# A planned attention and two-FFN kernel: pairs of PSUM banks taken early, and new numbers for the planner's pools and due times

## The chip, the core and the metric

One of the eight cores of a Trainium2 chip runs the whole program. The metric is device time in microseconds, start to end of the one launch. Its engines are PE (TensorE, matmuls), ACT (ScalarE), DVE (VectorE), POOL (GpSimd) and SP (SyncE, which only issues DMAs). Each runs its own list of instructions in the order in which they were written, and waits on semaphores for the others.

## What is computed

```
attention, per batch (2 batches of 12288 queries, C = 128):
  kv_pool = mean of 4x4 patches of kv           -> 768 keys
  k = v   = kv_pool @ w_sr
  x1      = softmax(q @ k.T / sqrt(C)) @ v
layer 1:  h = x1 @ w_in1 (128 -> 2048);  g = h * clip(h + 3, 0, 6) / 6;  x2 = g @ w_out1
layer 2:  h = x2 @ w_in2 (128 -> 2048);  g = h * cos(h);                 out = g @ w_out2
```

Inputs and output are float32.

## The kernel before

**Tiles.** The 24576 queries are cut into 48 blocks `b` of 512. A layer of a block is 8 units `p`; a unit is 256 of the 2048 hidden features, which fill a pair of PSUM banks (2 x 512 floats in each partition). Every float32 operand of a matmul is split into two float16 halves, `hi` and `lo`, and a product is three matmuls: hi·hi, lo·hi, hi·lo.

**A unit**, by its operations and lines: `ff_in` (PE, six matmuls of 512 columns, L1141 to L1143, into a pair of banks); in layer 1 `relu` (ACT, L1156) and `gate` (DVE, L1161), after which the pair is free; in layer 2 `turns` (ACT, L1166), `rest` (DVE, L1171), `sine` (ACT, L1177) and `times` (DVE, L1180), after which the pair is free; then `cast` to float16 `hi` (on ACT, L1186, or on POOL, L1188, whichever the planner finds sooner), `low` (POOL, L1191) and `ff_out` (PE, six matmuls, L1149 to L1151, into a single bank that gathers all 8 units of the block). Layer 2 runs 28 units behind layer 1 (`LAG`).

**Attention of a block.** Four `scores` (PE, L896, six matmuls each, into a pair of banks), each followed by `row_max` (DVE, L901 and L905) and `exp` (ACT, L911). Then there are two ways to turn the exponentials round for the product with the values:

- blocks below `BY_PE`: PE transposes them (`by_pe`, L999), ACT or DVE copies them out, and `values` (L1029) multiplies in float32; the queries are transposed by PE too (L778);
- all other blocks: DVE splits them into halves (`split`, L970 and L971), which frees the pair; SP stores them to DRAM (`store`, L977, tile `scr`), reads them back with three transposing DMAs (L1014, one for each third of the keys), and `values` (L1035) is three groups of six float16 matmuls, one behind each DMA. The queries go the same way (`power` and `up`, L796 to L818, `split` on POOL, L830 and L831, then DMAs).

**What sets the order.** The kernel is written as a list of about 8000 operations. `Plan.run` is a list scheduler that runs while the program is built: it walks through time with a fixed cost for every operation, gives each engine the ready operation of the lowest `prio` whose tiles are free, and so writes every engine's list. `prio` is the block's due time plus the offsets in the table of constants (`AV_AT` for `values`, `OUT_AT` for `ff_out`, and so on); operations more than `WINDOW` beyond the oldest open one may not start. Tiles come from pools of fixed size: `NW` float32 tiles, `NHI`, `NLO` and `NY` float16 ones, and the eight PSUM banks of the class `Banks`, from which an operation takes one bank or two neighbouring ones. On the chip nothing of this is decided again: only the lists and the semaphores are left.

Of the kernel before, what the change touches and what calls it, by code (L numbers as in the profile page):

```python
# [36 lines left out]
LAG = 28  # L37
AHEAD = 4

NW, NHI, NLO, NY = 16, 18, 18, 11  # L40
SPARE = 5

NSCR = 3

BY_PE = 6

VALUES = [[0], [1], [2]]

NBANKS = 8

NSUM = 5

# [6 lines left out]
TURNS = 2  # L59

POOL_PARTS = 16
RAWS = 8
ET_SPARE = 2

FIRST_SPARE, FIRST_BLOCKS = 0, 6


WINDOW = 150000.0
LOAD_AHEAD = 5000
Q_AHEAD = 20000  # L70
KV_AHEAD, KV_STEP, KV_PROJECT = 400000, 110000, 20000
KV_FIRST = 40000
IDLE_UNTIL = 10
WARM = 3
A_STEP = 1000
W_FIRST, W_STEP = 8000.0, 6000.0
HI_AT, LO_AT, OUT_AT = 12000, 8000, 20000
OUT_STEP = 1800
Q_AT, AT_AT, AV_AT, XS_AT = -1000, 4000, 20000, 20000
ACT_AT, DVE_AT, SIN_AT, MUL_AT = 4000, 200, -6000, -8000  # L80


BANKS = {"one": 1, "two": 2}
# [17 lines left out]
class Banks:  # L101
# [5 lines left out]

    def __init__(self, n):
        self.free = [True] * n

    def find(self, n):
        f = self.free
        if n == 1:
            at = [i for i in range(len(f)) if f[i]]
            return min(at, key=lambda i: (f[i ^ 1], i), default=None)
        at = [i for i in range(len(f) - 1) if f[i] and f[i + 1]]
        return max(at, key=lambda i: (i % 2 == 0, i), default=None)

    def pop(self, n):
        i = self.find(n)  # L120
        self.free[i : i + n] = [False] * n
        return i, n

    def append(self, taken):
        i, n = taken
        self.free[i : i + n] = [True] * n


class Plan:
# [24 lines left out]

    def lacks(self, tag, spare):
        if tag in BANKS:
            return self.slots[tag].find(BANKS[tag]) is None
        return len(self.slots[tag]) <= spare

# [3 lines left out]
    def run(self):  # L163
# [19 lines left out]
        events = [0.0]  # L183
# [4 lines left out]
        now = 0.0  # L188
        while started < len(self.ops):
            assert events, [  # L190
                (o.prio, o.where, o.take) for o in order if o not in begun and not todo[o]
            ][:20]
            now = max(now, heapq.heappop(events))
            while backs and backs[0][0] <= now:
                _, _, key = heapq.heappop(backs)
                tag, tile_ = self.held.pop(key)
# [5 lines left out]
            while again:  # L202
                again = False
                for e in sorted(queue):
# [3 lines left out]
                    while queue[e]:  # L208
                        item = heapq.heappop(queue[e])
                        o = item[2]  # L210
# [25 lines left out]
                    o = pick  # L236
# [16 lines left out]
                    heapq.heappush(events, o.end)  # L253
                    for key in o.drop:
                        heapq.heappush(backs, (o.seen, o.seq, key))
                    for u in users.get(o, ()):
                        todo[u] -= 1
                        if not todo[u]:
                            ready(u, max(a.seen for a in u.after))
                            heapq.heappush(events, ready_at[u])  # L260
# [4 lines left out]
def attention_ffn_ffn_kernel(  # L265
# [54 lines left out]

    free_banks = Banks(NBANKS)
    plan = Plan(
# [23 lines left out]

    banks = psum.tile([P, NBANKS, T], F32, name="banks")

# [415 lines left out]
    def plan_attention(prio, b):  # L764
# [80 lines left out]

        if b < BY_PE:
            a = op(prio - LOAD_AHEAD, {"dma": 1400}, load, take=[(raw, "w")])
# [16 lines left out]
        for j in range(NJ):  # L864
            a = plan_scores(prio + 1000 * j, b, j, [q_op, *k_ops], by_op)
            if b >= BY_PE:
                a, stored = plan_halves(prio + 1000 * j + 500, b, j, a, first)
# [7 lines left out]
        a = None  # L875
        for cps in [[cp] for cp in range(GK)] if b < BY_PE else VALUES:
            cp = cps[0]
            before = [a, *(parts[c] for c in cps)]
            if not cp:
                before += [v_32[0], v_32[1]] if b < BY_PE else v_ops  # L880
            a = plan_values(prio + AV_AT + 1300 * cp, b, cps, before, acc)
# [3 lines left out]
    def plan_scores(prio, b, j, before, by_op):  # L885
# [24 lines left out]
        def exp(e):  # L910
            nc.scalar.activation(  # L911
                flat(plan[e_])[:, 0:KEYS] if b < BY_PE else keys_of(ps), keys_of(ps), AF.Exp,
                bias=plan[nm][:, 0:1], scale=plan["qs", b][:, 2:3],
# [499 lines left out]
```

## Time and profile before

| | us |
|---|---|
| device time, median of 3 runs | 2563.74 (2561.98 to 2566.88) |
| device time of the profiled execution | 2567.5 |
| its span, first to last instruction | 2565.7 |
| PE busy | 2459.1 (96%) |
| ACT, DVE, POOL busy | 2256.9, 2203.1, 2080.4 |

A matmul's row in the trace is as long as the matmul is in the pipeline, longer than the distance to the next one's start. Where PE waits, the next row names in brackets how long the engine had no row, and who ended that.

### The profile page before, as it was taken

What the parts mean: (1) busy time and instruction counts of PE and PEld (TensorE: products, weight loads), DVE (VectorE), ACT (ScalarE), POOL (GpSimd) and SP (SyncE); (2) the same over time, 40 slices, a digit from 0 to 9 for tenths busy, and PEclk for the clock granted to TensorE, in tenths of its full rate; (3) what the DMA queues carried; (4) which work ended last, traced back from release to release, by engine and by line L of the source; (5) the groups of instructions that cost most, each with busy time, mean ns of one, the idle gap of its engine ahead of it and who ended that gap; (6) DMA issues with size and microseconds to landing.
All of it is one profiled execution on the core that took longest, in us unless ns stands there. A gap on an engine that the chain in (4) does not pass through costs nothing.

```text
span 2565.7 us, 33121 instructions
## 1 busy us (share of the span) xinstructions
PE 2459.1 (96%) x11616; PEld 1147.2 (45%) x11616; DVE 2203.1 (86%) x2775; ACT 2256.9 (88%) x2485; POOL 2080.4 (81%) x1231
## 2 busy tenths in 40 slices
PE   7999999999999999999999999999999999999998
PEld 5444444444444444444444444444444444444443
DVE  8977898888888888888888888889888888888887
ACT  4889888889888888898898989989998899988898
POOL 1998787888778787788778887888788888876888
PEclk9999999999999999999999999999999999999999
DMA  6201334553555334543345344543553455334401
GB/s 214 62 21 46 78 91 101 114 119 75 135 112 108 102 83 103 103 107 79 89 103 113 87 91 109 108 84 91 112 111 78 91 112 110 74 81 95 92 13 42
DMA packets 553514, 239.86 MB, mean 93 GB/s; under 512 B 370049, under 2 KB 524801, under 8 KB 553345
## 3 DMA queue, kind: packets, MB, share of 16 engines
q1 hardware_dynamic: 553344, 237.73, 41.1%
q8 instruction: 91, 1.49, 0.3%
q14 instruction: 79, 0.64, 0.1%
HBM read 46.20 MB, written 102.07 MB: 58 GB/s over the span
## 4 chain that ended last, share of the span: by engine, by line
PE 39%; DVE 18%; ACT 18%; DMA 13%; issue 6%; POOL 3%; SPq 3%; ACTq 0%; DVEq 0%; POOLq 0%
DMA w<-scr 8%; DVE w L1161 5%; PE banks L1149 5%; PE banks L1151 5%; PE banks L1150 5%; PE banks L1141 5%; PE banks L1143 5%; PE banks L1142 5%; DMA scr<-w 4%; PE banks L1035 4%; ACT w L1166 3%; ACT hi L1186 3%; ACT banks L911 3%; ACT w L1156 3%; PE banks L896 3%
## 5 line engine op out<-in xcount | busy, mean ns | idle before, releaser
L1191 POOL TENSOR_TENSOR lo<-w,hi 128x1024 f16<-128x1024 f32 x768 | 1620.8, 2136 | 154.4 <-ACT hi L1186 148.1
L1186 ACT CAST hi<-w 128x1024 f16<-128x1024 f32 x554 | 572.5, 1044 | 115.1 <-DVE w L1161 93.9
L1141 PE MATMUL banks<-y,w_in_hi 128*128 128x512 f16 x1536 | 583.3, 380 | 30.7 <-DVE w L1180 14.6
L1151 PE MATMUL banks<-lo,w_out_hi 128*128 128x512 f16 x1536 | 583.1, 380 | 8.5 <-POOL lo L1191 8.4
L1149 PE MATMUL banks<-hi,w_out_hi 128*128 128x512 f16 x1536 | 583.0, 380 | 3.2 <-DVE w L1180 2.3
L1142 PE MATMUL banks<-y,w_in_lo 128*128 128x512 f16 x1536 | 583.0, 380 | 0.0
L1143 PE MATMUL banks<-y,w_in_hi 128*128 128x512 f16 x1536 | 583.0, 380 | 0.0
L1150 PE MATMUL banks<-hi,w_out_lo 128*128 128x512 f16 x1536 | 582.7, 379 | 0.0
L1171 DVE SCALAR_TENSOR_TENSOR w<-banks,by,w 128x1024 f32<-128x1024 f32 x384 | 488.3, 1280 | 87.6 <-ACT w L1166 82.9
L1180 DVE SCALAR_TENSOR_TENSOR w<-w,banks 128x1024 f32<-128x1024 f32 x384 | 463.6, 1217 | 102.5 <-ACT w L1177 98.5
L1161 DVE SCALAR_TENSOR_TENSOR w<-w,banks 128x1024 f32<-128x1024 f32 x384 | 464.3, 1214 | 71.7 <-ACT w L1156 71.1
L1156 ACT ACTIVATE w<-banks,three,v_by 128x1024 f32<-128x1024 f32 x384 | 459.5, 1202 | 29.8 <-PE banks L1143 24.5
L1166 ACT ACTIVATE w<-banks,by 128x1024 int32<-128x1024 f32 x384 | 422.1, 1110 | 65.2 <-PE banks L1143 46.3
L1177 ACT ACTIVATE w<-w,quarter 128x1024 f32<-128x1024 f32 x384 | 436.2, 1148 | 21.6 <-DVE w L1171 14.8
L1188 POOL CAST hi<-w 128x1024 f16<-128x1024 f32 x214 | 220.7, 1039 | 206.5 <-PE banks L1151 85.5
L1142 PEld LDWEIGHTS <-w_in_lo 128*128 128x128 f16 x1536 | 150.2, 98 | 217.2 <-issue 56.2
L1141 PEld LDWEIGHTS <-w_in_hi 128*128 128x128 f16 x1536 | 150.2, 98 | 191.5 <-DVE w L971 16.9
L1143 PEld LDWEIGHTS <-w_in_hi 128*128 128x128 f16 x1536 | 150.3, 98 | 182.1 <-issue 1.4
L1151 PEld LDWEIGHTS <-w_out_hi 128*128 128x128 f16 x1536 | 150.3, 98 | 181.9 <-issue 1.1
L1149 PEld LDWEIGHTS <-w_out_hi 128*128 128x128 f16 x1536 | 150.4, 98 | 181.7 <-issue 13.0
L1150 PEld LDWEIGHTS <-w_out_lo 128*128 128x128 f16 x1536 | 150.4, 98 | 170.4 <-issue 5.6
L896 PE MATMUL banks<-k_hi,y 128*128 128x512 f16 (+1 forms) x768 | 201.7, 328 | 8.6 <-DVE w L1161 3.9
(119 smaller groups left out, 2425.6 us busy)
## 6 DMA issues: line engine op xcount, KB each, us to landing
scr<-w SPq DMA_DIRECT2D x168, 384.0 KB, 2.8
w<-in_kv_dram SPq DMA_DIRECT2D x24, 512.0 KB, 6.5
w<-in_q_dram SPq DMA_DIRECT2D x48, 256.0 KB, 2.9
w<-scri SPq DMA_DIRECT2D x48, 256.0 KB, 4.5
out_dram<-w SPq DMA_DIRECT2D x48, 256.0 KB, 3.2
scro<-w SPq DMA_DIRECT2D x47, 256.0 KB, 2.1
scrq<-w SPq DMA_DIRECT2D x42, 256.0 KB, 2.4
w<-in_moe_w_in_dram SPq DMA_DIRECT2D x8, 512.0 KB, 8.4
```

The lines of the kernel that those rows point to most:

```text
L1141: nc.tensor.matmul(t[:, i, :], w_hi[:, k, :], xx[:, 0, :], start=True, stop=False)
L1142: nc.tensor.matmul(t[:, i, :], w_lo[:, k, :], xx[:, 0, :], start=False, stop=False)
L1143: nc.tensor.matmul(t[:, i, :], w_hi[:, k, :], xx[:, 1, :], start=False, stop=True)
L1149: nc.tensor.matmul(t, o_hi[:, k, :], h[:, i, :], start=(k == 0), stop=False)
L1150: nc.tensor.matmul(t, o_lo[:, k, :], h[:, i, :], start=False, stop=False)
L1151: nc.tensor.matmul(t, o_hi[:, k, :], l[:, i, :], start=False, stop=(k == 2 * NP - 1))
L1156: nc.scalar.activation(plan[g], two(ps), AF.Relu, bias=three, scale=v_by[:, b // NBB, 3:4])
L1161: nc.vector.scalar_tensor_tensor(out=plan[g], in0=plan[g], scalar=6.0 * G1, in1=two(ps), op0=ALU.min, op1=ALU.mult)
L1166: nc.scalar.activation(plan[g].bitcast(I32), two(ps), AF.Copy, bias=0.25, scale=plan["by", b][:, 2:3])
L1171: nc.vector.scalar_tensor_tensor(out=plan[g], in0=two(ps), scalar=plan["by", b][:, 2:3], in1=plan[g].bitcast(I32), op0=ALU.mult, op1=ALU.s ...
L1186: nc.scalar.copy(plan[hi], plan[g])
L1191: nc.gpsimd.tensor_tensor(out=plan[lo], in0=plan[g], in1=plan[hi], op=ALU.subtract)
```

## The change

The class `Banks` keeps, for every bank, the time at which the planner expects it back (`soon`). A pair may be taken when its lower bank is free and its upper bank is free or due back within `LEAD` = 700 ns of the planner's clock; the claimed bank then goes over to the new owner. On the chip the fourth matmul of such a pair waits for the upper bank's reader by its semaphore, as any other does. Besides this the table of constants changes: pool sizes, `BY_PE` from 6 to 4, the window and the due times.

```diff
-NW, NHI, NLO, NY = 16, 18, 18, 11
+NW, NHI, NLO, NY = 18, 15, 15, 13
-BY_PE = 6
+BY_PE = 4
+LEAD = 700
-RAWS = 8
+RAWS = 5
-WINDOW = 150000.0
+WINDOW = 60000.0
-Q_AHEAD = 20000
-KV_AHEAD, KV_STEP, KV_PROJECT = 400000, 110000, 20000
+Q_AHEAD = 45000
+KV_AHEAD, KV_STEP, KV_PROJECT = 600000, 180000, 40000
-HI_AT, LO_AT, OUT_AT = 12000, 8000, 20000
-OUT_STEP = 1800
-Q_AT, AT_AT, AV_AT, XS_AT = -1000, 4000, 20000, 20000
-ACT_AT, DVE_AT, SIN_AT, MUL_AT = 4000, 200, -6000, -8000
+HI_AT, LO_AT, OUT_AT = 12000, 8000, 36000
+OUT_STEP = 1400
+Q_AT, AT_AT, AV_AT, XS_AT = -1000, 4000, 32000, 32000
+ACT_AT, DVE_AT, SIN_AT, MUL_AT = 2000, 200, -3000, -4000
...
+    def near(self, i):
+        return self.free[i] or (
+            i in self.soon and i not in self.claimed and self.soon[i] <= self.now + LEAD
+        )
...
-        at = [i for i in range(len(f) - 1) if f[i] and f[i + 1]]
-        return max(at, key=lambda i: (i % 2 == 0, i), default=None)
+        at = [i for i in range(len(f) - 1) if f[i] and self.near(i + 1)]
+        return max(at, key=lambda i: (f[i + 1], i % 2 == 0, i), default=None)
...
                     for key in o.drop:
                         heapq.heappush(backs, (o.seen, o.seq, key))
+                        tag, tile_ = self.held[key]
+                        if tag in BANKS:
+                            for j in range(tile_[0], sum(tile_)):
+                                self.slots[tag].soon[j] = o.seen
```

The lines of the program move down by 23 behind this (L1141 becomes L1164, L1035 becomes L1058, L1186 becomes L1209). The numbers reorder every engine's list. Three places are shown, all in block 36, in the middle of the run, where one block's list repeats the last one's.

PE at the first two of the three groups of `values` (before: L1035, after: L1058; the rows between the first and the last of a unit are left out). Before, one `ff_in` of layer 2 stands between the groups:

```order
L1143 MATMUL banks_188<-y6_143,w_in2_hi_81 128x512
L1035 LDWEIGHTS v_hi_74
...
L1035 MATMUL banks_188<-w6_91,v_hi_74 128x512
L1141 LDWEIGHTS w_in2_hi_81
...
L1143 MATMUL banks_188<-y6_143,w_in2_hi_81 128x512
L1035 LDWEIGHTS v_hi_74
L1035 MATMUL banks_188<-w7_92,v_hi_74 128x512
```

Of the change, there are two, and an `ff_out` of layer 1 ahead of the first group:

```order
L1174 MATMUL banks_186<-lo3_121,w_out1_hi_79 128x512
L1058 LDWEIGHTS v_hi_74
...
L1058 MATMUL banks_186<-w16_101,v_hi_74 128x512
L1164 LDWEIGHTS w_in2_hi_81
...
L1166 MATMUL banks_186<-y12_145,w_in2_hi_81 128x512
L1164 LDWEIGHTS w_in2_hi_81
...
L1166 MATMUL banks_186<-y12_145,w_in2_hi_81 128x512
L1058 LDWEIGHTS v_hi_74
L1058 MATMUL banks_186<-w3_88,v_hi_74 128x512
```

The second and third groups stand one unit later, counted from the last `scores` of the block; the first stands where it stood.

ACT at the units 0 to 3 of layer 2 of this stretch, behind the switch to the sine's table. Before:

```order
L1177 ACT_TABLE_LOAD
L1177 ACTIVATE w15_100<-w15_100,quarter_66 128x1024
L1177 ACTIVATE w0_85<-w0_85,quarter_66 128x1024
L1156 ACTIVATE w10_95<-banks_188,three_64,v_by_68 128x1024
L1186 CAST hi0_101<-w0_85 128x1024
L1186 CAST hi4_105<-w10_95 128x1024
L1166 ACTIVATE w3_88<-banks_188,by2_150 128x1024
L1156 ACTIVATE w13_98<-banks_188,three_64,v_by_68 128x1024
L818 ACTIVATE w8_93<-w8_93,qs4_161 128x512
L1177 ACTIVATE w3_88<-w3_88,quarter_66 128x1024
```

Of the change:

```order
L1179 ACTIVATE w10_95<-banks_186,three_64,v_by_68 128x1024
L1200 ACT_TABLE_LOAD
L1200 ACTIVATE w15_100<-w15_100,quarter_66 128x1024
L1200 ACTIVATE w12_97<-w12_97,quarter_66 128x1024
L1209 CAST hi0_103<-w15_100 128x1024
L1189 ACTIVATE w0_85<-banks_186,by2_148 128x1024
L1209 CAST hi5_108<-w12_97 128x1024
L1179 ACTIVATE w13_98<-banks_186,three_64,v_by_68 128x1024
L1200 ACTIVATE w0_85<-w0_85,quarter_66 128x1024
```

A `cast` (L1209, before L1186) that POOL had (L1188) now stands on ACT, between a `turns` (L1189) and a `relu` (L1179); the queries' `up` (L818) is elsewhere. In the whole list ACT has 622 of the 768 casts, before 554.

DVE behind the last `split` of the block's exponentials. Before:

```order
L971 SCALAR_TENSOR_TENSOR w9_94<-banks_188,w9_94 128x3x256
L939 RECIPROCAL s5_173<-s5_173 128x4
L1171 SCALAR_TENSOR_TENSOR w15_100<-banks_188,by2_150,w15_100 128x1024
L1171 SCALAR_TENSOR_TENSOR w0_85<-banks_188,by2_150,w0_85 128x1024
L1180 SCALAR_TENSOR_TENSOR w15_100<-w15_100,banks_188 128x1024
L1180 SCALAR_TENSOR_TENSOR w0_85<-w0_85,banks_188 128x1024
L1161 SCALAR_TENSOR_TENSOR w10_95<-w10_95,banks_188 128x1024
```

Of the change:

```order
L994 SCALAR_TENSOR_TENSOR w9_94<-banks_186,w9_94 128x3x256
L962 RECIPROCAL s1_167<-s1_167 128x4
L1114 TENSOR_REDUCE by4_150<-banks_186 128x1
...
L1194 SCALAR_TENSOR_TENSOR w15_100<-banks_186,by2_148,w15_100 128x1024
L1194 SCALAR_TENSOR_TENSOR w12_97<-banks_186,by2_148,w12_97 128x1024
L1135 SCALAR_TENSOR_TENSOR y5_138<-banks_186,by4_150,y5_138 128x512
L1184 SCALAR_TENSOR_TENSOR w10_95<-w10_95,banks_186 128x1024
L1203 SCALAR_TENSOR_TENSOR w15_100<-w15_100,banks_186 128x1024
L1203 SCALAR_TENSOR_TENSOR w12_97<-w12_97,banks_186 128x1024
```

The scaling of layer 1's result (L1114 to L1135) has come in here, and the `gate` (L1184) stands ahead of the two `times` (L1203) and not behind them.

## Rows read from the trace of the kernel before

**Rows 1.** The page: busy us, share of the span, instructions

```profile
PE 2459.1 (96%) x11616; PEld 1147.2 (45%) x11616; DVE 2203.1 (86%) x2775; ACT 2256.9 (88%) x2485; POOL 2080.4 (81%) x1231
```

**Rows 2.** Windows: stretch, length, PE, PEld, DVE, ACT, POOL busy, PE clock, DMA share, GB/s

```profile
0.00:200.00 200.00, 176.51 (x860) 97.77 (x861) 170.94 (x315) 151.01 (x197) 147.15 (x106) 0.97 0.31 98
300.00:1300.00 1000.00, 957.01 (x4529) 442.05 (x4529) 864.17 (x1068) 879.02 (x966) 806.65 (x475) 1.00 0.46 103
1300.00:2300.00 1000.00, 974.91 (x4601) 447.13 (x4600) 876.10 (x1069) 902.98 (x980) 836.43 (x490) 1.00 0.45 97
1843.80:1893.80 50.00, 49.68 (x237) 22.84 (x236) 44.73 (x56) 45.88 (x51) 42.58 (x25) 1.00 0.44 101
2500.00:2565.70 65.70, 55.84 (x248) 24.35 (x245) 47.55 (x40) 55.66 (x57) 53.98 (x31) 0.95 0.14 41
```

**Rows 3.** Waits of PE, whole span: us in total, times, longest

```profile
PE banks L1035 <- DMA w<-scr: 35.7, 34, 2.3
PE banks L1141 <- DVE w L1180: 14.6, 16, 1.6
PE banks L1141 <- DVE w L1161: 12.9, 35, 0.9
PE banks L1151 <- POOL lo L1191: 8.4, 7, 2.2
```

**Rows 4.** PE in order of time, blocks 26, 37, 44: start, length, what, [idle before]

```profile
1333.17 0.38 PE L1141 MATMUL banks<-y,w_in_hi 128*128 128x512 f16 x1
...
1893.81 0.38 PE L1141 MATMUL banks<-y,w_in_hi 128*128 128x512 f16 x1
...
1909.43 0.38 PE L1141 MATMUL banks<-y,w_in_hi 128*128 128x512 f16 x1
...
1910.72 0.38 PE L1035 MATMUL banks<-w,v_hi 128*128 128x512 f16 x1
...
1912.50 0.38 PE L1141 MATMUL banks<-y,w_in_hi 128*128 128x512 f16 x1 [0.32 <-DVE w L1161]
...
1915.52 0.38 PE L1035 MATMUL banks<-w,v_hi 128*128 128x512 f16 x1 [1.56 <-DMA w<-scr]
...
2251.47 0.38 PE L1141 MATMUL banks<-y,w_in_hi 128*128 128x512 f16 x1
```

**Rows 5.** SP in order of time, the same block: its stores and transposing reads

```profile
1900.75 0.37 SPq L977 DMA_DIRECT2D scr<-w  x1
...
1908.61 6.31 SPq L1014 DMA_TRANSPOSE w<-scr  x2
```

**Rows 6.** DMAs of the page: KB where known, median us from issue to landing

```profile
scr<-w SPq DMA_DIRECT2D x168, 384.0 KB, 2.8
w<-scr SPq DMA_TRANSPOSE x126, 4.9
```

**Rows 7.** PE in order of time, the attention of early blocks done by PE

```profile
47.25 0.66 PE L778 MATMUL banks<-ident,w 128*128 128x128 f32 x4 [0.52 <-ACT w L818]
47.74 3.60 PE L1029 MATMUL banks<-w,v_all 128*128 128x512 f32 x8
51.18 1.04 PE L999 MATMUL banks<-ident,w 128*128 128x128 f32 x8
```

**Rows 8.** ACT in order of time around the wait at 1912.5

```profile
1909.90 1.20 ACT L1156 ACTIVATE w<-banks,three,v_by 128x1024 f32<-128x1024 f32 x1
```

**Rows 9.** DVE in order of time, the same stretch

```profile
1899.73 0.96 DVE L971 SCALAR_TENSOR_TENSOR w<-banks,w 128x768 f16<-128x768 f32 x1
...
1911.24 1.21 DVE L1161 SCALAR_TENSOR_TENSOR w<-w,banks 128x1024 f32<-128x1024 f32 x1
```

**Rows 10.** Groups by line: busy us, mean ns of one, idle before and its releasers

```profile
L1186 ACT CAST hi<-w 128x1024 f16<-128x1024 f32 x554 | 572.5, 1044 | 115.1 <-DVE w L1161 93.9 <-DVE w L1180 16.9
L1188 POOL CAST hi<-w 128x1024 f16<-128x1024 f32 x214 | 220.7, 1039 | 206.5 <-PE banks L1151 85.5 <-DVE w L1180 84.6 <-DVE w L1161 30.4
```

**Rows 11.** Waits of PE from 0 to 200 us: us in total, times, longest

```profile
PE banks L583 <- DVE sum L575: 7.0, 2, 6.7
```

More of the change, by code (lines that the diff above doesn't have):

```diff
@@ L109, in __init__ @@
         self.free = [True] * n
+        self.soon = {}
+        self.claimed = set()
+        self.now = 0.0
+    def near(self, i):
+        return self.free[i] or (
+            i in self.soon and i not in self.claimed and self.soon[i] <= self.now + LEAD
+        )
     def find(self, n):
@@ L115, in find @@
             return min(at, key=lambda i: (f[i ^ 1], i), default=None)
-        at = [i for i in range(len(f) - 1) if f[i] and f[i + 1]]
-        return max(at, key=lambda i: (i % 2 == 0, i), default=None)
+        at = [i for i in range(len(f) - 1) if f[i] and self.near(i + 1)]
+        return max(at, key=lambda i: (f[i + 1], i % 2 == 0, i), default=None)
     def pop(self, n):
         i = self.find(n)
-        self.free[i : i + n] = [False] * n
+        for j in range(i, i + n):
+            if not self.free[j]:
+                self.claimed.add(j)
+            self.free[j] = False
         return i, n
@@ L125, in append @@
         i, n = taken
-        self.free[i : i + n] = [True] * n
+        for j in range(i, i + n):
+            self.soon.pop(j, None)
+            if j in self.claimed:
+                self.claimed.remove(j)
+            else:
+                self.free[j] = True
 class Plan:
@@ L156, in lacks @@
         if tag in BANKS:
+            self.slots[tag].now = self.now
             return self.slots[tag].find(BANKS[tag]) is None
@@ L192, in run @@
             ][:20]
-            now = max(now, heapq.heappop(events))
+            now = self.now = max(now, heapq.heappop(events))
             while backs and backs[0][0] <= now:
```

## The prediction

> **What bounds the kernel now.** I read the page first. PE has rows in 96% of the span, ACT 88%, DVE 86%, POOL 81% [rows 1]: four busy engines, and PE is the one that all work passes through. The windows show where PE stands idle: 23.5 us of the first 200, 43 us from 300 to 1300, 25 us from 1300 to 2300, 10 us of the last 66, at full clock nearly throughout [rows 2]. So there is no stage with another bound; in each, PE runs with small holes. The timeline of one block shows a hole closely [rows 4]. Six matmuls of 512 columns take 1.29 us (1909.43 to 1910.72), 0.216 each, but a row lasts 0.38. A wait therefore begins 0.16 us before the bracket's count: [0.32] is a hole of 0.48, [1.56] one of 1.72. With 0.16 added for each, the view of waits [rows 3] reads: for the transposed exponentials of `values` 35.7 + 34 x 0.16 = 41 us; for a pair whose last reader is the layer-1 `gate` (L1161) 12.9 + 35 x 0.16 = 18.5 us; for a pair held by the layer-2 `times` (L1180) 17 us; for `low` halves 9.5 us. Those four, 86 us, are what a better order can win in the middle; the first 200 us wait for other things [rows 11].
>
> **The change, part by part.** *The pair taken early.* In the built order I count the pairs that are taken while the upper bank is still held: 6 of 978, all within the first five blocks. Elsewhere banks 0-1, 2-3 and 6-7 go round as fixed pairs and both halves come back together, so a free lower bank under a busy upper one does not occur. Each of the 6 can bring at most the lower bank's three matmuls forward, 3 x 0.216 = 0.65 us; 6 make 4 us, in a stretch where a wait of up to 6.7 us stands elsewhere. I take 0, with ends 0 and -4. What moves the time is the table of numbers.
>
> *Two blocks from PE to DMA (`BY_PE` 6 to 4).* By PE a block costs 24 transposes, 8 to a row of 1.04 us [rows 7], of which some 0.17 is the pipeline's end, so 2.6; 12 `values` matmuls, of which 8 take 3.44 us (47.74 to 51.18), so 5.2; and 0.5 for the queries (47.25 to 47.74): 8.3 us. By DMA it costs 18 x 0.216 = 3.9. Two blocks: -8.7 us of PE, if PE would not have waited there anyway. What the two add, 8 splits on DVE and 18 DMAs on SP, falls on engines with idle time, at some 200 us; without that cover the 8 splits, two rows of 0.96 us each [rows 9], would cost 15.
>
> *`values` one unit later.* Block 37 shows the chain. The last `scores` end at 1893.81; the last split lies on DVE until 1900.69 [rows 9], its store is issued at 1900.75, and the second and third of its reads from 1908.61 on [rows 5]. The first group of `values` starts at 1910.72, unhindered; the second waits until 1915.52, 21.7 us behind the scores and 6.9 behind its read's issue [rows 4]. The second group's read is what is late. By the order before, it stands 19.4 us of matmuls behind the scores; in the new order 20.8, since the first group stays where it was and two `ff_in` lie between. That is so in 32 of 44 blocks, and SP's list from the last store to the three reads is the same in nearly all. The mean of the 34 waits is 41 / 34 = 1.2 us, the longest 2.5. A shift of 1.3 us would leave some 6 us in all; but the hole at 1912.50 [rows 4] sits ahead of it and goes as well (next part), which makes the net shift 0.8 and would leave 15. I take 12 left, so -29; ends -35 (all but a few long ones) and -12 (the chain is later by 0.8 us because splits run later).
>
> The Trainium skill would price this otherwise. The rows say: 2.8 us for a store and 4.9 for a transposing read [rows 6]. The page "Advanced Engine Details and Errata", X-Bar Transpose (TRN2), states that transposing DMAs are as fast as ordinary ones. By it the second read would land 2.1 us sooner, the 34 waits would not exist and the term would be 0; the waits are in the trace, so the rows decide.
>
> *Pairs of banks.* At 1912.50 an `ff_in` takes a pair whose last `ff_in` ended two units, 2.59 us, before. `relu` began at 1909.90 [rows 8] and `gate` at 1911.24 [rows 9], lasting 1.21, so the pair was free 0.48 late: a layer-1 pair needs about 3.1 us. I counted such distances in both orders, leaving out the ends of the run: 57 of 2.59 us before, 8 or so now, since most are 3.89 now (an `ff_out` stands between, as in the place shown). That takes 18.5 x 49/57 = 16 us. Distances of 5.2 us or less behind a layer-2 `ff_in`, the short ones for its four steps: 22 before, 3 now; I take 9 of the 17 us, as the rest also occurs at longer distances. Against this, the new order has 34 `ff_in`, before 11, that take the pair of a block's last `scores` 6.54 us behind it, while the split ended 6.88 behind: 0.4 us each, +9. Net -16; ends -28 (the 9 do not come, or are shorter) and 0.
>
> *68 casts from POOL to ACT*, 1.04 us each [rows 10]: +71 us on ACT, -71 on POOL. In block 36, a window of 50 us, ACT has 45.9 us of rows [rows 2]; the repeating block gets two casts more, 48 us. PE's matmuls of a block are 49.3 us (16 units of 2.59, four `scores` of 0.97, three groups of 1.29), so ACT stays below it, if not by much. I take 0, covered by the 115 us that ACT waited in front of its casts [rows 10]; uncovered it is +71. By the rows PE is the engine that all wait for, at 96% [rows 1]. [...]
>
> *`low` halves.* `OUT_AT` puts `ff_out` later: the distance from a layer-1 `ff_in` to its `ff_out` was 14.9 us in the middle and 6.2 at the least, and is 23.9 and 8.7. The 9.5 us of waits for POOL's `low` should nearly go: -8; ends -9.5 and -4. The smaller pools `NHI` and `NLO` (15 for 18) hold this, because a float16 tile lives for about 9 units.
>
> *The start.* Five raw weight tiles in flight and not eight, another order of scores and weights: I cannot price it from rows of another order. The holes are 23.5 us [rows 2]; I take 0 and half of them, 12, either way.
>
> **Sum.** Against the profiled execution, 2567.5: -8.7 - 29 - 16 - 8 = -62; 2505.5. That execution lies 3.8 us above the median of the three runs, so **2502**.
>
> **The rivals.**
> - *The waits come back elsewhere.* PE runs ahead and finds ACT and DVE, now fuller, late at other pairs. For: ACT waits for DVE and DVE for ACT all through [rows 10], and several new distances fit by 0.1 to 0.2 us. Against: the short distances are gone, not moved. Only the PE work and the `low` term then stay, 2567.5 - 17 = 2550, **2547** on the median. Chance 0.12.
> - *The order's new numbers cost nothing and bring nothing*, the title's mechanism being idle: PE saves 8.7 and the start takes it back, **2563**. It would need every one of the four waits to be unchanged in sum. Chance 0.03.
> - *ACT sets the pace* (slower). The place is the one shown on ACT: a cast now stands before a `turns` and a `relu`, whose pairs come free later by one cast. If each of the 68 delays PE, and the gains at `values` and at the pairs are lost: 2567.5 - 8.7 - 8 + 71 = 2622, **2618**. It decides from the point where ACT's casts of a block no longer fit into its idle time, 50 - 46 = 4 us, that is from four added casts; the repeating block gets two. Chance 0.05. [...]
>
> **How the numbers follow.** The forecast has 0.80. Its own bounds: all good ends together (-4 - 8.7 - 35 - 28 - 9.5 - 12) give 2467, which I cut at 2478 as they will not all meet; all bad ends (-8.7 - 12 - 0 - 4 + 12) give 2551 on the median. I set 2478 to 2546, which leaves out most of the first rival. The smallest change that a measurement of this kernel tells from none is about 0.2%, 5 us: the runs shown lie that far apart. Faster: the forecast 0.80, the first rival 0.12, less a little for what I have not thought of: 0.90. Same 0.04, slower 0.06.
>
> **What would show it.** PE's rows for L999, L778 and L1029 by a third fewer; waits of L1058 for `scr` at 5 to 15 us; waits of L1164 for `gate` under 5 us, and new ones of about 0.4 us behind `split` (L994), some 30 of them; hardly any for `low`; the last `scores` of two blocks 50.0 to 50.4 us apart in the second half, before 51.0 as the mean of 18 (1333.17 to 2251.47 [rows 4]); ACT at 92 to 93% and POOL at 80%. Wrong would be: waits for the DMAs as before, although later in the list (then a store or SP is later too); PE waiting for `times` or `gate` in most units (first or third rival); a first 200 us with 35 us of holes or more.

## The result, and the profile after

The changed kernel takes 2534.2 us (median of four, 2532.8 to 2535.8) against 2562.9 for the kernel before (2559.3 to 2566.9) beside it: a ratio of 0.9888, interval 0.9871 to 0.9905, 29 us less. Forecast were 61 less. The direction was right, the size less than half.

The profiled execution takes 2535.0, its span is 2533.2. The page's busy line, answering to [rows 1]:

```profile
PE 2459.1 (97%) x11572; PEld 1136.5 (45%) x11572; DVE 2212.2 (87%) x2789; ACT 2294.4 (91%) x2545; POOL 2019.4 (80%) x1167
```

The same windows as in [rows 2], with the same columns:

```profile
0.00:200.00 200.00, 175.36 (x848) 93.44 (x849) 176.54 (x312) 147.42 (x194) 141.74 (x103) 0.97 0.38 113
...
300.00:1300.00 1000.00, 973.36 (x4593) 447.49 (x4592) 878.15 (x1082) 915.03 (x1007) 795.64 (x456) 1.00 0.45 102
1300.00:2300.00 1000.00, 990.21 (x4645) 450.66 (x4644) 883.29 (x1090) 931.56 (x1029) 802.90 (x455) 1.00 0.46 100
```

The gain lies in the two middle windows, where PE's idle time by rows fell from 43 to 27 us and from 25 to 10. The first 200 us lost one. PE's waits over the whole span, answering to [rows 3] (us in total, times, longest):

```profile
PE banks L1164 <- DVE w L994: 15.6, 46, 2.8
PE banks L1058 <- DMA w<-scr: 8.1, 10, 1.3
...
PE banks L919 <- DVE w L994: 5.4, 21, 0.3
...
PE banks L1164 <- DVE w L1184: 1.9, 7, 0.5
...
PE banks L1164 <- DVE w L1203: 1.6, 4, 0.6
...
PE banks L1174 <- POOL lo L1214: 1.1, 2, 0.6
```

All four waits that the prediction wanted gone are nearly gone: the transposed exponentials 35.7 to 8.1, `gate` 12.9 to 1.9, `times` 14.6 to 1.6, `low` 8.4 to 1.1. On top stands a wait that the view before had no great part of: `ff_in` (L1164) and `scores` (L919) wait for the second half of a `split` (L994), that is for a pair of banks that scores held. Before, these two rows read:

```profile
PE banks L1141 <- DVE w L971: 2.2, 5, 0.6
...
PE banks L896 <- DVE w L971: 0.3, 1, 0.3
```

PE in order of time shows two of these waits in one block of the change:

```profile
1916.29 0.38 PE L1174 MATMUL banks<-lo,w_out_hi 128*128 128x512 f16 x1
1916.94 0.39 PE L919 MATMUL banks<-k_hi,y 128*128 128x512 f16 x1 [0.27 <-DVE w L994]
...
1926.86 0.22 PE L1108 MATMUL banks<-ident_b,col 128*128 128x128 bf16 x1
1927.24 0.38 PE L1164 MATMUL banks<-y,w_in_hi 128*128 128x512 f16 x1 [0.17 <-DVE w L994]
```

The bracket says 0.27; from start to start it is 0.65 where 0.216 is usual, a hole of 0.43. Many holes of this size have no bracket at all, since the longer row before them covers them. So for an account I took, for every matmul of the trace, the distance to the next one's start less the usual distance of its kind (the lowest tenth). This gives the time of all matmuls at their usual distance, and holes by place:

| us | before | changed | difference | forecast |
|---|---|---|---|---|
| matmuls at their usual distance | 2406.8 | 2398.1 | -8.7 | -8.7 |
| holes ahead of `values` | 41.0 | 10.8 | -30 | -29 |
| holes for `low` | 11.5 | 1.5 | -10 | -8 |
| pairs that layers 1 and 2 held | 42.0 | 16.7 | -25 | -16 - 9 = -25 |
| pairs that scores held | 7 | 43.6 | **+37** | +9 |
| all else (start and end above all) | | | +4 | 0 |
| span | 2565.7 | 2533.2 | -32.5 | -62 |

(The holes at pairs are those behind 200 us. "All else" is what is left to the span.) Five rows came within 4 us of the forecast. One, the last part of "pairs of banks", came 28 us worse, and that is the miss.

Of these 44 us, 17 are at the pair of a block's last scores, 13 at that of its first, 13 at that of its third. They are not of one kind. Take the matmuls at their usual distance, from the end of the scores to the matmul that takes their pair next, in the 40 blocks 6 to 45:

- The last scores' pair is taken 6.5 us behind them in 32 blocks, before in 10 (mostly 7.7); the hole is 0.3 us each time, 10 us in all. Here the distance became shorter. The rest is at a few takes that are nearer still.
- The first scores' pair is taken 6.1 us behind them in 33 blocks, before in 25, with holes of 12.1 us now and of 0.1 before. Here the same distance no longer suffices.
- The third scores' pair is taken 6.1 us behind them in 33 blocks in both orders, with holes of 5.5 us now and 2.7 before; in 5 blocks of the change it is taken 3.6 or 4.8 us behind them, which holds 6.4 us.

For the first scores ACT shows why, in order of time:

```profile
1910.36 1.21 ACT L1179 ACTIVATE w<-banks,three,v_by 128x1024 f32<-128x1024 f32 x1
1911.46 1.05 ACT L1209 CAST hi<-w 128x1024 f16<-128x1024 f32 x1
1912.52 1.28 ACT L934 ACT_TABLE_LOAD   x1
1913.82 0.96 ACT L934 ACTIVATE banks<-banks,s,qs 128x768 f32<-128x768 f32 x1
```

The first scores' maximum was there at 1911.90, but ACT was in an unbroken row of `relu` and `cast` since 1904.25. It began the table load for `exp` at 1912.52, 0.62 us behind the maximum, and `exp` at 1913.82. Before, the maximum of a block's first scores is there at 1885.87 and the load begins 0.09 us behind it:

```profile
1884.80 1.03 ACT L1186 CAST hi<-w 128x1024 f16<-128x1024 f32 x1
1885.96 1.28 ACT L911 ACT_TABLE_LOAD   x1
1887.25 0.96 ACT L911 ACTIVATE banks<-banks,s,qs 128x768 f32<-128x768 f32 x1
```

Over blocks 25 to 43 `exp` begins 3.40 us behind the end of the first scores, before 2.85, and the split ends 6.46 behind them, before 5.98. The rows of the casts, by line, show what came onto ACT:

```profile
L1209 ACT CAST hi<-w 128x1024 f16<-128x1024 f32 x622 | 648.6, 1045 | 121.4 <-DVE w L1184 105.9 <-DVE w L1203 14.3
...
L1211 POOL CAST hi<-w 128x1024 f16<-128x1024 f32 x146 | 151.5, 1038 | 194.2 <-DVE w L1184 131.4 <-DVE w L1203 37.1 <-DVE s L962 10.9
```

In a repeating block four casts came over (units 0 and 7 of both layers) and two went to POOL (units 3 and 6 of layer 1). Two of the four, layer 2's last unit and layer 1's first, stand in that row ahead of `exp`.

### The profile page after: what moved, and what is told of

It reads as the page before. It is cut to its first block, busy times and chain, and to the rows that moved or that the text cites. A ratio compares the mean times of both kernels' runs of the same rounds, so it can differ in the third digit from the quotient of the medians.

```text
span 2533.2 us, 33111 instructions
## 1 busy us (share of the span) xinstructions
PE 2459.1 (97%) x11572; PEld 1136.5 (45%) x11572; DVE 2212.2 (87%) x2789; ACT 2294.4 (91%) x2545; POOL 2019.4 (80%) x1167
## 4 chain that ended last, share of the span: by engine, by line
ACT 31%; DVE 23%; PE 21%; issue 14%; POOL 5%; DMA 4%; SPq 1%; POOLq 0%; ACTq 0%; DVEq 0%
ACT hi L1209 9%; ACT w L1179 7%; DVE w L993 6%; ACT w L1189 5%; DVE w L1184 5%; ACT w L1200 4%; PE banks L1164 4%; POOL lo L1214 4%; PE banks L1058 4%; PE banks L1166 3%; PE banks L1165 3%; DVE w L994 3%; DVE w L1194 3%; DMA w<-scr 3%; DVE w L1203 2%
## 5 line engine op out<-in xcount | busy, mean ns | idle before, releaser
L1209 ACT CAST hi<-w 128x1024 f16<-128x1024 f32 x622 | 648.6, 1045 | 121.4 <-DVE w L1184 105.9
L1164 PE MATMUL banks<-y,w_in_hi 128*128 128x512 f16 x1536 | 583.9, 380 | 23.3 <-DVE w L994 15.6
L1184 DVE SCALAR_TENSOR_TENSOR w<-w,banks 128x1024 f32<-128x1024 f32 x384 | 465.0, 1215 | 78.0 <-ACT w L1179 77.3
L1203 DVE SCALAR_TENSOR_TENSOR w<-w,banks 128x1024 f32<-128x1024 f32 x384 | 464.0, 1217 | 26.7 <-ACT w L1200 22.6
L1179 ACT ACTIVATE w<-banks,three,v_by 128x1024 f32<-128x1024 f32 x384 | 460.9, 1204 | 10.7 <-PE banks L1166 10.1
L1189 ACT ACTIVATE w<-banks,by 128x1024 int32<-128x1024 f32 x384 | 424.6, 1115 | 13.6 <-PE banks L1166 10.2
L1211 POOL CAST hi<-w 128x1024 f16<-128x1024 f32 x146 | 151.5, 1038 | 194.2 <-DVE w L1184 131.4
L1164 PEld LDWEIGHTS <-w_in_hi 128*128 128x128 f16 x1536 | 150.2, 98 | 205.7 <-DVE w L994 31.8
L919 PE MATMUL banks<-k_hi,y 128*128 128x512 f16 (+1 forms) x768 | 209.1, 329 | 16.7 <-DVE w L994 5.4
```

The costliest lines, as they stand in the source:

```text
L1164: nc.tensor.matmul(t[:, i, :], w_hi[:, k, :], xx[:, 0, :], start=True, stop=False)
L1179: nc.scalar.activation(plan[g], two(ps), AF.Relu, bias=three, scale=v_by[:, b // NBB, 3:4])
L1184: nc.vector.scalar_tensor_tensor(out=plan[g], in0=plan[g], scalar=6.0 * G1, in1=two(ps), op0=ALU.min, op1=ALU.mult)
L1189: nc.scalar.activation(plan[g].bitcast(I32), two(ps), AF.Copy, bias=0.25, scale=plan["by", b][:, 2:3])
L1209: nc.scalar.copy(plan[hi], plan[g])
```

## The experiments

The orders below are the planner's own: its list is collected, edited in one place, and then emitted, so that nothing is planned anew (where it is, that is said). Of each edit only the lines that choose the place are shown. The runs were on four chips. On each the kernel before takes 2546.8 to 2547.6, 16 us less than beside the first comparison, while the changed kernel takes 2531 on the one of the four where it ran. So the experiments are held against these two numbers; for the changed kernel on the other three that is an assumption, and a difference of less than about 5 us is not told from none. Which chip the first comparison ran on is not known.

**The control, and the kernel before once more.** No edit.

> The changed kernel with no edit, beside the three that follow on the same chip, so that they are compared with it there. Both theories: 0.989 of the kernel before, as in the first comparison. If it comes out nearer 0.995, the differences between chips are as large as the effects asked after, and only kernels of one chip are to be compared.

Measured 2530.9 (2528.6 to 2531.4), ratio 0.9934 (0.9922 to 0.9947): here the change is worth 16 us, not 29.

> The kernel before with no edit, for a profile on this chip, where its runs take some 16 us less than those beside the first comparison (2547 against 2563), while the changed kernel takes nearly the same on both (2531 against 2534). If the difference is in its transfers, the waits of the values for the scores' transposed halves are less than the 41 us of the first profile (some 25), and the pairs' waits are the same; if it lies in the engines, all groups of holes are smaller alike.

This one run took 2543.0. Its waits of PE (line numbers of before):

```profile
PE banks L1141 <- DVE w L1180: 14.8, 16, 1.6
PE banks L1141 <- DVE w L1161: 12.4, 33, 0.9
PE banks L1035 <- DMA w<-scr: 12.2, 19, 1.6
```

Only one of [rows 3] is different: the transposed exponentials, 12.2 for 35.7; by holes 17.7 for 41.0. That is 23 of the 24.5 us between the spans. The three reads of a block each hold SP's queue for 2.68 us on average here, for 2.84 in the first trace (126 rows each; the changed kernel's 2.77 and 2.83, 132 rows). Up to the stores the two traces agree: over blocks 25 to 43 the last split ends 6.73 us behind the last scores and its store goes out at 6.79, in both. The second read lands at 19.95 here and at 20.70 there. So the difference comes in with the transfers. The term for `values` is right as the first trace gave it, but its size hangs on how fast the transfers are; the changed kernel depends on them less (holes of 5.5 us in the control's trace, 10.8 in the first).

It also shows where the change gains. Here the last scores of two blocks are 50.3 us apart between blocks 26 and 44, in the first trace 51.0, and with the change 50.6 in both traces. Against the control's trace (of another chip) the change has won 13.0 us by block 26, loses 5.4 of them up to block 44, and wins 4.3 behind it. By these two traces the new order is the slower one in the repeating stretch, where the transfers come in time.

**The pair rule alone undone**, planned anew:

```diff
-LEAD = 700
+LEAD = -1e9
```

> The changed kernel with the pair rule taken back (LEAD far below zero), all other numbers of the change kept. Theory (the rule acts on 6 pairs in the first blocks and the numbers do the rest): the time of the changed kernel, 2534 us, within 8 us, since the list is planned anew. Rival (the early pair carries the gain): back towards 2560 us.

2538.2 (2536.4 to 2540.0), 7 us above the changed kernel. How much of this is the rule itself is not shown, since the list as a whole comes out a little different.

**Six blocks on PE and not four**, planned anew:

```diff
-BY_PE = 4
+BY_PE = 6
```

> The changed kernel with six blocks transposed on TensorE as before, in place of four, planned anew. The two blocks' 44 matmuls of TensorE take 8.7 us by their distance in the trace. Theory: 2537 to 2542, 6 to 11 us more than the changed kernel, all of it ahead of 300 us. If it is the same or faster, the start waits for the transfers that take their place, and the term was worth nothing.

2536.8 (2535.2 to 2538.2), 6.0 more: the lower end. Matmuls at their usual distance are again 2406.8, 8.7 more, but the holes of the first 200 us are 30 and not 32: with four blocks the start takes a part back.

**`values` moved alone**: the order of before, the second and third group of `values` one unit later in 42 blocks.

```diff
+        for n in (g[2], g[1]):
+            i, j = pe[n], pe[n + 1]
+            if names[j][0] == "ff_in" or names[j][0] == "ff_out":
+                behind.setdefault(j, []).append(seq[i])
```

> The lists of the kernel before, but the second and third group of values stand one unit later on PE in all 42 blocks; nothing else is changed. By the term of the prediction (29 of the 41 us of waits go): 2534 us. Rival W (PE comes earlier to the pairs and waits there): half or less, 2548 us or more.

2577.2, ratio 1.0121 (1.0107 to 1.0135): 30 us slower than before. The waits of PE:

```profile
PE banks L1200 <- DVE w L1239: 48.7, 58, 1.6
PE banks L1200 <- DVE w L1220: 15.8, 41, 0.9
```

No wait for a transfer is among the long ones: the holes ahead of `values` are down to 2 us, lower than the term had them. But the `ff_in` that go ahead of `values` find their pairs still held by `times` (L1239) and `gate` (L1220). What the move is worth hangs on the other engines' order: the new list has it and 30 us less of holes ahead of `values` in the first trace, and alone it costs 30.

**The casts alone.** In the order of before, those two casts of a block go to ACT where POOL has them. That is 60 in all, 30 of each unit, and not the 80 that were expected (ACT's casts go from 554 to 614). The other way round, in the changed order, 80 go back to POOL. The edit of the first run:

```diff
+        if n == "cast" and e == "pool" and 6 <= k[2] and (k[1], k[3]) in ((2, 7), (1, 0)):
+            seq[i] = o, "act"
```

> The kernel before in its own order, with the two casts of a block that the change moved from GpSimd to ScalarE (80 of them) moved in the same way and nothing else. Theory A: the exponentials of the first scores start some 0.5 us later, and waits of 0.3 us appear 40 times at the pair of the first scores, as in the changed kernel: 8 to 15 us more than the kernel before. Theory B: before has the waits on values and on ScalarE's slack to take this up: ScalarE has 10% free, the time changes by less than 5 us. If it gets faster, GpSimd held the queries or low halves before.

2576.6, ratio 1.0115 (1.0099 to 1.013): 30 us slower. The term "I take 0, covered" was wrong in that order. It is not only the first scores' pair: PE waits for `gate` 26.2 us in 59 waits, where before had 12.4 in 33.

```profile
PE banks L1190 <- DVE w L1210: 26.2, 59, 0.9
```

> The changed kernel's lists, row for row, but 80 casts (unit 7 of layer 2 and unit 0 of layer 1, the two that stand ahead of a block's first exp) go from ACT back to POOL at the same place. Theory C (the casts on ACT delay exp, so split, so the pairs of the scores): the 13 us of PE's waits for the pair of the first scores go, 2519 to 2525 us. Rival W (PE now runs ahead and the holes only change their place): 2529 to 2539 us. Rival P (POOL is too full in that stretch): slower than 2539 us.

2527.3 (2525.0 to 2533.7), ratio 0.9925 (0.991 to 0.994): 4 us under the changed kernel, which the intervals don't tell from none. The holes at the first scores' pair are gone (13.7 to 1.7 between `ff_out` and `scores`), but the wait for the transposed exponentials is 17.2 us in 22 waits, where the changed kernel has 8.1 in 10 in its first trace and 4.0 in 7 in the control's. What takes its place had to be found.

**`exp` ahead of the cast.** In the changed order, in 41 blocks, the cast shown above at 1911.46 goes behind the first scores' `exp`:

```diff
+        if names[i][0] == "cast" and names[j][0] == "exp" and names[j][1][2] == 0 and names[j][1][1] >= 4:
+            swap[j] = i
```

> The changed kernel's own order, with one edit: in the 41 places where a cast stands right ahead of the first scores' exponential on ScalarE, the exponential goes ahead of that cast. Nothing is added or taken away. Theory A (the scores' pairs are waited for because ScalarE works off casts ahead of the exponential, so that the first scores' split ends late): the split ends about 0.5 to 1 us earlier, the 40 short waits of the scores that take the first scores' pair (13 us in all) go, and nothing else is held, since the cast's tile is wanted some microseconds later: 10 to 13 us less than the changed kernel. Theory B (the kernel moves at the pace of all engines together, a hole that is closed opens elsewhere): the waits move to another pair or to the casts' tiles, within 4 us of the changed kernel.

2550.0 (2545.8 to 2554.6): 19 us **slower** than the changed kernel. Both theories fail by size. Its waits of PE (numbers moved by 52):

```profile
PE banks L1110 <- DMA w<-scr: 31.5, 40, 2.0
...
PE banks L971 <- DVE w L1046: 0.5, 2, 0.3
```

The scores wait no longer (0.5; the control's trace, of the same chip, has 6.8), but `values` wait 31.5 (the control 4.0). Nothing of `values` was touched. POOL in order of time, in the changed kernel first (`lo` are the `low` halves, L853 the queries' split):

```profile
1904.42 10.49 POOL L1214 TENSOR_TENSOR lo<-w,hi 128x1024 f16<-128x1024 f32 x5 [1.53 <-PE banks L1174]
...
1918.04 0.61 POOL L853 CAST w<-w 128x512 f16<-128x512 f32 x1
```

and with `exp` first, where the cast ended at 1925.56:

```profile
1925.65 2.14 POOL L1266 TENSOR_TENSOR lo<-w,hi 128x1024 f16<-128x1024 f32 x1 [2.95 <-DVE w L1045]
...
1930.92 0.61 POOL L905 CAST w<-w 128x512 f16<-128x512 f32 x1
```

POOL takes its work in order. It stands 2.95 us until the moved cast has made its tile (the bracket names a `split`, but this row is the `low` of the unit whose cast was moved), and so the split of the queries, which is behind it, begins 4.3 us behind the block's first store below and not 1.1. It goes to SP, which takes its work in order too. SP in the changed kernel:

```profile
1916.91 2.24 SPq L1000 DMA_DIRECT2D scr<-w  x2
1919.92 0.37 SPq L859 DMA_DIRECT2D scrq<-w  x1
1924.14 1.19 SPq L867 DMA_TRANSPOSE y<-scrq  x1
1925.38 0.58 SPq L1000 DMA_DIRECT2D scr<-w  x1
...
1933.05 2.13 SPq L1037 DMA_TRANSPOSE w<-scr  x1
```

with `exp` first:

```profile
1926.64 2.31 SPq L1052 DMA_DIRECT2D scr<-w  x2
1932.80 0.37 SPq L911 DMA_DIRECT2D scrq<-w  x1
1935.11 1.19 SPq L919 DMA_TRANSPOSE y<-scrq  x1
1936.35 0.57 SPq L1052 DMA_DIRECT2D scr<-w  x1
...
1944.04 1.84 SPq L1089 DMA_TRANSPOSE w<-scr  x1
```

Counted from the first store, the queries' write goes out at 6.2 us and not at 3.0, their read 2.3 us behind it (it has to wait until the write has landed), the third store of the scores' halves at 9.7 and not 8.5, the first transposing read for `values` at 17.4 and not 16.1. This is a third theory (C): the queries' two transfers, which the new numbers put among the stores, stand ahead of the third store, and any delay of POOL reaches `values` through them. Over blocks 25 to 43 the third split ends 3.7 to 3.8 us behind the last scores in all three orders, but its store goes out at 4.1 us in the changed kernel, at 6.0 with `exp` first and at 5.5 with the casts back on POOL. So theory C covers the casts back as well: there the casts delay the queries' split themselves.

**The queries' transfers later.** A first try moved both, write and read, behind the next one or two stores, with the casts back on POOL:

```diff
+        at = [r for r in stores if b < r < min(users)][:2]
+        if at and at[-1] - b < 150:
+            behind[at[-1]] = [a, b]
```

> The changed kernel with the 80 casts back on GpSimd, as in the second run, and the queries' two transfers on SyncE's queue moved behind the next one or two stores of the scores' halves in 41 blocks. Theory A (with the casts back the scores' pairs come free in time, and the values waited again only since SyncE, which works in order, stood at the queries that GpSimd now splits later): the waits at the first scores' pair stay away and those at the values fall from 17 us to 8 or less, 10 us less than the changed kernel. Theory B: GpSimd's low halves and queries are late by themselves, or a new wait comes: no less than the run with the casts alone, within 5 us of the changed kernel.

2642.0, ratio 1.0367 (1.0348 to 1.0387). Waits of PE, and of SP's queue:

```profile
PE banks L1123 <- DMA w<-scr: 99.8, 55, 3.7
```

```profile
SPq L932 <- DMA scrq<-w: 119.8, 42, 4.3
```

Now SP stands in all 42 blocks, 2.9 us each, until the queries' write has landed, and behind it stand the transfers that `values` need. What has to go is the read alone, to behind the block's last transposing read; the write stays. Three runs on one chip have that edit, with `exp` first, with the casts back, and by itself:

```diff
+        if e == "dma" and names[b][0] == "back" and of(o, "qt"):
+            at = [r for r in reads if b < r < min(users)][:3]
+            if at and at[-1] - b < 200:
+                behind[at[-1]] = [b]
```

> The changed kernel with the first scores' exponential ahead of the cast, as in the run of that name, and on SyncE's queue the queries' transposing read back (not their write) behind the block's last transposing read of the scores' halves. Theory C (the exponential's move made GpSimd's low halves and with them the queries' split 2 us later; the queries' write and read stand on SyncE's queue ahead of the third store of the scores' halves, and the read also waits there until the write has landed; so the values' halves came late): the third store goes out some 3 us earlier than with the exponential's move alone, the waits at the values fall from 31 us to 8 or less, those at the first scores' pair stay away, and the time is some 10 us under the changed kernel. Theory B (the holes belong to a loop of all engines, and an edit only moves them): the time stays within 5 us of the changed kernel or above it, with waits of another kind.

2517.8 (2515.9 to 2519.8), ratio to before 0.9886 (0.9873 to 0.99). SP in order of time, and the waits of PE:

```profile
1904.32 2.31 SPq L1068 DMA_DIRECT2D scr<-w  x2
1910.46 0.37 SPq L927 DMA_DIRECT2D scrq<-w  x1
1911.70 0.37 SPq L1068 DMA_DIRECT2D scr<-w  x1
...
1918.66 1.94 SPq L1105 DMA_TRANSPOSE w<-scr  x1
...
1927.06 1.30 SPq L935 DMA_TRANSPOSE y<-scrq  x1
```

```profile
PE banks L1126 <- DMA w<-scr: 6.5, 7, 1.8
...
PE banks L987 <- DVE w L1062: 0.8, 3, 0.3
```

The write still goes out at 6.1, but the third store follows at 7.4 and the first read at 14.3. Over blocks 25 to 43 the third store goes out 3.9 us behind the last scores, again right behind its split. Both waits are gone at once: 31.5 to 6.5 for `values`, and the scores' 0.8.

> The changed kernel with the 80 casts back on GpSimd and the queries' read back behind the block's last transposing read of the scores' halves. Theory C: the waits at the values fall from the 17 us of the run with the casts alone to 8 or less, the first scores' pair is not waited for, some 10 us under the changed kernel. Theory B: the time stays within 5 us of the changed kernel or above it. In the run in which write and read both went later, SyncE stood for the landing of the write directly ahead of the reads of the halves; here the write stays where it was, so that this wait should not come.

2516.8 (2516.1 to 2519.1), ratio 0.9884 (0.987 to 0.9897); waits for `values` 6.3 in 9.

> The changed kernel with the queries' read back behind the block's last transposing read of the scores' halves, and nothing else. Theory C: the third store goes out about 1 us earlier, but the fourth waits for the last split anyway, so the values gain 0 to 4 us and the scores' pairs nothing: 0 to 5 us under the changed kernel. Theory B: the same time within 2 us. Slower by more than 5 us would mean that the queries themselves come late.

2531.4 (2528.0 to 2533.3), ratio 0.9936 (0.9922 to 0.9949): the changed kernel's time. So the read's place costs nothing as long as POOL is in time, and without it neither edit for the first scores' pair brings a gain that is clear of noise; against this run, on the same chip, each of the two brings 14 to 15 us together with it, as much as the holes at that pair. The two versions are faster than both kernels.

**The other two pairs.** First an `ff_out` ahead of the `ff_in` that takes the last scores' pair, in 35 blocks of the changed order:

```diff
+                if names[i][0] == "ff_in" and names[j][0] == "ff_out" and freed[2] == 3:
+                    behind[j] = i
```

> The changed kernel's lists, but in 35 blocks the ff_in that takes the pair of the block's last scores and the ff_out behind it change places on PE, so that 7.83 us of matmuls and not 6.54 lie between. Theory O (the place is one unit too early; its 0.44 us each is lost for good): 12 to 15 us faster than the changed kernel, 2519 to 2522 us. Rival W (a later wait takes over): 2529 us or more.

2578.7, ratio 1.0127 (1.011 to 1.0144), 48 us above the changed kernel. Waits of PE:

```profile
PE banks L1219 <- DVE w L1258: 33.8, 36, 1.0
PE banks L1227 <- DVE by L1169: 20.1, 36, 4.1
```

The `ff_out` now waits for a bank that layer 1's scaling still reads (L1169), and a later `ff_in` for `times` (L1258). Then, with the order kept, the last split's second half no longer reads the pair: from block 8 on it writes zeros, in the second run for the third scores too.

```diff
+            if b >= 8 and j >= 3:
+                return nc.vector.memset(low, 0.0)
```

> The changed kernel in its own order; from block 8 on, the second half of the last scores' split (the low parts, 0.96 us on VectorE, which read the pair of banks) is replaced by writing zeros, so that the low parts of a quarter of the weights are left out. The pair comes free about 1 us earlier; all other instructions and their order stay. Theory D (the pairs of scores are waited for because their splits end too late for the shorter distance, and that wait is a price of its own): the 40 holes behind the last split, 17 us, go, and the time falls by 12 to 17 us. Theory B (a hole closed there opens at the next pair or at the values): the holes behind the last split go, others of about the same sum come, and the time stays within 5 us of the changed kernel's 2531.

2524.7 (2523.0 to 2525.1): 6 us less. By who held the pair, against the control's trace, the holes at the last scores' pair fell from 17.2 to 3.9 us and those at the third's stayed (12.9 and 12.8), but those at layer 1's pairs rose from 9.3 to 15.8 and at layer 2's from 8.9 to 11.7. Nearly all of the first rise is at one place: unit 6 of layer 1 takes the last scores' pair, and the next `ff_in` that takes it, unit 2 of layer 2, now waits for unit 6's `gate` (0.7 to 6.9 us in 35 blocks). PE comes to that pair earlier, and the `gate` stays where it was. On DVE that `gate` begins some 1.0 us behind the end of its `relu`, with a row of layer 1's scaling right ahead of it in 34 of 36 blocks.

> As the run before, with the low parts of the third scores left out as well (from block 8 on half of the weights have no low parts). Theory D: the holes behind the third split (17 us in 39 takes on this chip) go too, 25 to 34 us less than the changed kernel, some 2500. Theory B: within 5 us of the changed kernel, since VectorE's order and the layers' pairs set the pace.

2512.9 (2512.8 to 2513.4): 18 us less than the changed kernel. The third scores' pair now has holes of 2.2 us, the last's of 4.6, layer 1's pairs of 16.5 and layer 2's of 7.5. Each run lies between its two theories: of the 13.3 us that were closed at the last pair 9.3 came back at the layers' pairs, while the 10.6 us closed at the third's brought 12. VectorE's rows are 23 and 47 us less in these two as well, since zeros are written faster than the halves; a part of the gain can be that, and no run keeps the two apart.

## Why the prediction was right and wrong

- **The failed step** is the one that ends "0.4 us each, +9. Net -16" under *pairs of banks*. Net it was +12 (-25 and +37). I looked at one of the four scores of a block, and there at the distance alone. For the pair of the last scores the reading was right: 32 takes at the 6.5 us that I had, with 0.3 us each, and a few nearer ones; its holes grew by 14.5 us for my 9. The pairs of the first and the third scores came to another 22 us (4 before, 26 now) that the sum did not have. There the usual distance is 6.1 us in both orders, so that a count of new distances, as I made it, would have found little more than the 5 early takes at the third (6.4 us). At the first scores it is the release that moved: `exp` begins 0.55 us later and the split ends 0.48 us later.
- **What made half of it** stands in the step behind it: "68 casts from POOL to ACT ... I take 0". I held ACT's busy time against the block's length. The casts did not fill ACT; they stood ahead of `exp`, and the pair of the first scores is freed by what comes behind `exp`. The runs with `exp` first and with the casts back show 14 to 15 us for it, once the way to `values` is free. For the third scores no run shows why their split ends later; in the trace a `gate` stands ahead of their maximum on DVE and a cast ahead of their `exp`, which is argued only.
- **The rival "the waits come back elsewhere"** was given 0.12 and 2547. The truth lies between it and the forecast: half of the gain came back, and in the rival's way, PE running ahead and finding other pairs still held. Every edit of one part shows its force: `values` alone +30, casts alone +30, `exp` first +19, an `ff_out` first +48.
- **`values`, `low`, two blocks fewer and the layers' pairs** came out within 2 us of their terms in the profile; in time the two blocks are worth 6.0 and not 8.7. The size of `values` holds for the first comparison only: where the kernel before has holes of 17.7 us there and not 41, the term has at most 18 to win, which is most of why the same change gives 0.9934 there. The price of 0 that the prediction sets beside this term does not follow: it held the landing of a 384 KB store against that of a transposing read of 512 KB (the four stores of a block come back in three reads), and an ordinary read of 512 KB lands after 6.5 us in the same trace (`w<-in_kv_dram`), the transposing one after 4.9.
- **ACT sets the pace** did not happen as I put it: ACT has 91%, PE 97%. 80 casts fewer on ACT gave 4 us alone, which is not clear of noise, and 15 with the queries' read later. But `exp` first leaves ACT's load as it is and gives 14 with the same read, so the place in its list is what counted here. The Trainium skill's page "Perfetto Trace Analysis", Identifying the Most-Contended Engine, names two measures for PE, MFU (matmul work against the peak) and the share of its weight loads. They point apart here: the weight loads have 45%, less than ACT's 91%, while the matmuls at their usual distance fill 2398.1 of 2533.2 us, 95%, which, as far as that distance is PE's full rate, is an estimate of MFU and puts PE first.
- **The pair rule** I took at 0 with an end of -4; undone it costs 7 us in a list planned anew. (The built list has 975 takes of a pair and not 978; 6 of them are early, as said.)
- **Shown by the profile as written**: casts 622, POOL 80%, waits for `values` 8.1 us, holes of 0.2 to 0.4 us behind `split` (but some 100 of them and not 30), `gate` and `low` nearly without waits. Off: ACT has 91%, not 92 to 93; blocks are 50.6 us apart (blocks 26 to 44, last scores), not 50.0 to 50.4; before 51.0.

What stays open: why the split of the third scores ends later, and whether DVE's list ahead of unit 6's `gate` is all that brings most of the last pair's holes back. I have no run that moves a row of DVE alone.

## What to carry to other kernels

When an order is changed, hold every buffer's distance against its release, for all who hold it, not for the holder that the change brings to mind, and read both anew: a distance that stays the same can become too short when the release moves. An engine with time to spare still delays what stands behind its new work, which is to be looked up in its list and not in its share. A store followed by its read back on one in-order queue holds all behind it until the store has landed (2.9 us in each of 42 blocks here), so the read belongs behind everything urgent. Where an edit closes a wait and the time doesn't fall, look for the queue through which it reached the next: here ACT to POOL to SP to PE, each in order.

## What the runs showed of the hardware

The same kernel before took 2562.9 us beside the first comparison and 2546.8 to 2547.6 on the four chips of the experiments. PE's matmuls are alike in the two traces of it (380 and 379 ns on average for L1141), the splits end at the same place, and the transposing reads hold SP's queue for 2.84 and 2.68 us. I had not expected transfers to differ between two runs of one program by so much that the worth of a change does (29 us and 16).
